# VectorE instead of negated copies and adding DMAs for one chunk's low parts, in a gated attention and GEGLU kernel

## The chip, the cores and the metric

The kernel runs on one core of a Trainium2 chip, as one program. The metric is the device time of one execution in microseconds; the median of three runs stands for a kernel. Names of engines: PE is TensorE, PEld its weight loads, DVE is VectorE, ACT is ScalarE, POOL is GpSimd, SP is SyncE.

## The reference

For 2048 tokens of width 512, two branches are computed from the same `x` and mixed by a sigmoid gate per token:

```python
x = A_x
g = _sigmoid((x * gate_w).sum(-1, keepdims=True))
a = _A_ref(x, A_wqkv, A_wo)        # 32 heads of 16; each token sees 8 keys, 2 apart
b = (_gelu(x @ w_gate) * (x @ w_up)) @ w_down     # F = 1792
return g * a + (1 - g) * b
```

All data is float32.

## The kernel before

**Numbers in two parts.** Each float32 operand of a matmul is held as a high part (a copy rounded to `F32R`) and a low part (the value less the high part). A product takes three matmuls: high by high, high by low, low by high.

**Two parities.** The tokens are split by parity into two halves of 1024. For each half the program makes queries and keys, then values, then runs the feed-forward branch over `FC` = 14 chunks of 128 hidden columns (`ffn(par)`, with `gate_up` per chunk). The products with `w_gate` and `w_up` use Strassen-Winograd sums over two token blocks, so a chunk has seven products (`product`, L781), and ends with two hidden tiles of 128 by 512, key `(f, 0)` and `(f, 1)`. `down` (L830) multiplies the hidden tiles of two chunks at a time by their rows of `w_down`; the last pair, chunks 12 and 13, is multiplied at the end of `ffn(1)`.

**Hidden tiles.** `hidden` (L797 to L807) multiplies GELU by up on VectorE (L797, tile `c`) and makes the two parts `hh` and `hl` in one of two ways. Where the chunk's number is not in `LOWS[par]`, ScalarE copies to `hh` (L800) and VectorE subtracts for `hl` (L801). Where it is, ScalarE writes the negated tile to `hl` (L805), a DMA that POOL issues adds the tile to it in memory (L806), and ScalarE copies to `hh` (L807).

**Attention beside it.** Attention runs on VectorE while TensorE does the feed-forward work. `pull` gives out its steps by a credit, behind the other work in priority. A unit is 128 channels of one parity. `mix` forms the value products (L585), folds them (L589, L591, L593), transposes half a unit (L598) and stores it by four DMAs on SP (L600). The second parity's last unit loads its values (`v`, L523 and L524) into the buffer of the unit before, so when that unit's last L585 is over.

**The end.** `out_first` multiplies the first parity's attention output by `wo` (L1062, tiles `A` and `S` as weights) while the second parity's units finish. `channels` loads half a unit back (L1040, `raw<-os`), splits it (ACT L90 for `hh`, DVE L91 for `hl`), and `finish` multiplies it into the accumulators. The program's last work is that chain for the last half unit, then four groups of three matmuls, a copy to `rt` or `s`, and the store of the output.

**Order.** A scheduler puts each engine's instructions in order from priorities and its own estimates of when operands are ready; at run time each engine takes them strictly in this order and waits on semaphores. A moved instruction can therefore move its neighbours.

Of the kernel before, what the change touches and what calls it, by code (L numbers as in the profile page):

```python
# [36 lines left out]
PIPE = 4  # L37
BT = 4
MASKED = -1e9 * DH ** 0.5
LOWS = (4, 8, 10), (4, 6, 8, 10, 12)  # L40


GROUPS = (("t1", "t2", "b11"), ("b21", "t3", "b22", "t4"))
# [5 lines left out]
def tile_gated_mix(ctx: ExitStack, tc: tile.TileContext, xt, wqkv, wff, wo, out):  # L49
# [11 lines left out]
    def tl(tag, dt=F32):  # L61
        return pool.tile([P, COLS.get(tag, 512)], dt, name=tag, bufs=BUFS[tag])
# [733 lines left out]
    def hidden(par, key, ge, up):  # L796
        nc.vector.tensor_tensor(ge, ge, up, op=OP.mult)  # L797
        hh_, hl_ = tl("hh", F32R)[:, :512], tl("hl", F32R)[:, :512]
        if key[0] not in LOWS[par]:
            END[:] = [nc.scalar.activation(hh_, ge, AF.Copy),  # L800
# [555 lines left out]
```

## Time and profile before

| quantity | value |
|---|---|
| median of three runs | 592.74 us (592.54 to 600.27) |
| profiled execution | 592.89 us, of which 591.1 us from the first to the last instruction |
| granted TensorE clock | 1.000 |
| busy: PE | 585.7 us (99%) |
| busy: DVE | 535.0 us (91%) |
| busy: ACT | 425.3 us (72%) |
| busy: POOL | 126.8 us (21%) |

The span is counted from the first instruction; 1.8 us of the profiled execution lie outside it. In the timeline, a row gives start, length, engine, line, operation, tiles and count, and in brackets the idle time of the engine ahead of the instruction and what ended it. An instruction's end can lie behind the next one's start, since an engine overlaps neighbours that don't wait for each other.

### The profile page before, as it was taken

Reading aid. Unit: us, or ns where it says so; the run is one execution under the profiler, and the core shown is the slowest. Engines: PE = TensorE matmul, PEld = TensorE weight load, DVE = VectorE, ACT = ScalarE, POOL = GpSimd, SP = SyncE. Lnnn points to the kernel's source line nnn. Section 1 sums busy time; section 2 is a strip of 40 time slices with the busy share of each in tenths; the row PEclk is TensorE's granted clock in tenths of the full one; section 3 lists DMA queues with packets and bytes.
Section 4 is the critical chain, followed back from the end, with each engine's and each line's share of the span. In section 5 each row is a group of like instructions: output and inputs, shape, how many; then the busy total and the mean of one; then the engine's idle time right before and its main releaser. Section 6 shows DMA issues by size and latency. Waiting matters only on the chain.

```text
span 591.1 us, 8266 instructions
## 1 busy us (share of the span) xinstructions
PE 585.7 (99%) x2743; PEld 489.1 (83%) x2743; DVE 535.0 (91%) x628; ACT 425.3 (72%) x752; POOL 126.8 (21%) x153
## 2 busy tenths in 40 slices
PE   9999999999999999999999999999999999999997
PEld 7889888888888888888889888888888888887885
DVE  6989998999899995998997999998999899989882
ACT  6778667778887779786687655768776967796522
POOL 0140751112111212113120761112121212112200
PEclk9999999999999999999999999999999999999999
DMA  8789999978987979899989999969798989548915
GB/s 305 228 247 281 301 310 231 296 197 238 289 222 218 273 205 273 224 264 347 284 231 380 222 272 269 277 162 257 178 263 224 254 213 247 144 111 227 202 44 178
DMA packets 87848, 141.71 MB, mean 240 GB/s; under 512 B 8575, under 2 KB 49919, under 8 KB 87806
## 3 DMA queue, kind: packets, MB, share of 16 engines
q1 hardware_dynamic: 65454, 103.21, 52.2%
q0 software_dynamic: 22064, 37.59, 34.6%
q8 instruction: 21, 0.34, 0.2%
q10 hardware_dynamic: 288, 0.39, 0.2%
q14 instruction: 21, 0.17, 0.1%
HBM read 69.83 MB, written 46.49 MB: 197 GB/s over the span
## 4 chain that ended last, share of the span: by engine, by line
PE 96%; ACT 2%; DMA 1%; issue 0%; SPq 0%; DVE 0%; ACTq 0%
PE p L781 44%; PE p L830 13%; PE acc L830 12%; PE acc L478 11%; PE p L1062 6%; PE p L364 4%; PE acc L364 3%; PE p L478 2%; PE acc L1062 2%; DMA raw<-xt 1%; ACT A L90 0%; ACT L898 0%; ACT g L135 0%; ACT hl L805 0%; ACT hh L807 0%
## 5 line engine op out<-in xcount | busy, mean ns | idle before, releaser
L781 PE MATMUL p<-S,g 128*128 128x512 f32 x672 | 167.0, 389 | 0.0
L781 PEld LDWEIGHTS p<-S,g 128*128 128x128 f32 x672 | 125.8, 188 | 25.8
L781 PE MATMUL p<-A,g 128*128 128x512 f32 x504 | 125.8, 389 | 0.0
L781 PEld LDWEIGHTS p<-A,g 128*128 128x128 f32 x504 | 94.4, 188 | 19.8 <-ACT rt L845 0.4
L585 DVE TENSOR_TENSOR prod<-v,lg 128x2048 f32<-128x2048 f32 x32 | 72.8, 2274 | 1.4 <-DMA v<-vs 1.2
L542 DVE TENSOR_REDUCE lg<-prod 128x128 f32<-128x2048 f32 x32 | 73.0, 2280 | 0.2
L539 DVE TENSOR_TENSOR prod<-kq 128x2048 f32<-128x2048 f32 x32 | 72.9, 2277 | 0.2
L830 PE MATMUL p<-d,hh 128*128 128x512 f32 x224 | 68.6, 390 | 0.3 <-ACT p L824 0.3
L830 PE MATMUL acc<-d,hh 128*128 128x512 f32 x224 | 59.7, 389 | 0.0
L740 POOL DMA_DIRECT2D g<-raw x26 | 23.6, 907 | 161.1 <-ACT g L737 103.6
L792 ACT ACTIVATE c<-p 128x512 f32<-128x512 f32 x56 | 33.4, 597 | 33.7 <-PE p L781 33.6
L830 PEld LDWEIGHTS p<-d,hh 128*128 128x128 f32 x224 | 41.9, 188 | 9.5 <-ACT p L824 0.8
L830 PEld LDWEIGHTS acc<-d,hh 128*128 128x128 f32 x224 | 42.0, 188 | 8.7
L793 DVE TENSOR_TENSOR c<-c,s 128x512 f32<-128x512 f32 x56 | 37.8, 681 | 5.5 <-ACT c L792 5.2
L830 PE MATMUL p<-d,hl 128*128 128x512 f32 x112 | 42.1, 389 | 0.0
L797 DVE TENSOR_TENSOR c<-c 128x512 f32<-128x512 f32 x56 | 38.1, 683 | 1.3 <-ACT c L898 1.2
L589 DVE TENSOR_TENSOR prod<-prod 128x1024 f32<-128x1024 f32 x32 | 39.0, 1217 | 0.1
L845 ACT ACTIVATE rt<-p 128x512 f32<-128x512 f32 x48 | 27.8, 596 | 15.0 <-PE p L830 14.8
L786 ACT ACTIVATE s<-p 128x512 f32<-128x512 f32 x56 | 33.2, 594 | 5.3 <-PE p L781 4.9
L478 PE MATMUL acc<-d,S 128*128 128x512 f32 x144 | 35.5, 390 | 0.1
L830 PE MATMUL acc<-d,hl 128*128 128x512 f32 x112 | 35.1, 389 | 0.0
L772 POOL DMA_DIRECT2D d<-r x23 | 19.8, 860 | 68.9 <-ACT d L771 41.6
(222 smaller groups left out, 1062.3 us busy)
## 6 DMA issues: line engine op xcount, KB each, us to landing
g<-raw POOLq DMA_DIRECT2D x26, 512.0 KB, 6.7
ws<-g SPq DMA_DIRECT2D x14, 768.0 KB, 5.9
g<-ws SPq DMA_DIRECT2D x14, 768.0 KB, 6.7
r<-wff SPq DMA_DIRECT2D x28, 256.0 KB, 4.4
raw<-wff SPq DMA_DIRECT2D x14, 512.0 KB, 4.6
d<-r POOLq DMA_DIRECT2D x23, 256.0 KB, 6.7
ws<-raw SPq DMA_DIRECT2D x14, 384.0 KB, 5.8
raw<-ws SPq DMA_DIRECT2D x14, 384.0 KB, 4.0
```

Source lines behind the costliest of these rows:

```text
L364: LAST[:] = [nc.tensor.matmul(ps[:, :n], x[:, ts], VO[b][w][:, kc * WQ:kc * WQ + n], start=first, stop=(kc == 1 and i == 2), skip_group_ch ...
L478: LAST[:] = [nc.tensor.matmul(ps, x[:, ts], w, start=(start and kc == i == 0), stop=(kc == 1 and i == 2), skip_group_check=True)]
L539: paced(nc.vector.tensor_tensor(prod, spans(k, jj), q[:, jj:jj + 2, None, :].to_broadcast([P, 2, W, UC]), op=OP.mult))
L542: nc.vector.tensor_reduce(two_of(lg, jj), prod.rearrange("p j w (h d) -> p (j w) h d", d=DH), axis=AX.X, op=OP.add)
L585: paced(nc.vector.tensor_tensor(prod.rearrange("p j w (h d) -> p (j w) h d", d=DH), spans(v, jj).rearrange("p j w (h d) -> p j w h d", d=D ...
L589: nc.vector.tensor_tensor(prod[:, :, :4], prod[:, :, :4], prod[:, :, 4:], op=OP.add)
L781: LAST[:] = [nc.tensor.matmul(ps, w_, a_, start=(start and kc == 0 and n == 0), stop=(kc == 1 and n == 2), skip_group_check=True)]
L792: nc.scalar.activation(c, ps, AF.Copy)
L793: nc.vector.tensor_tensor(c, c, s, op=OP.add)
L797: nc.vector.tensor_tensor(ge, ge, up, op=OP.mult)
L830: LAST[:] = [nc.tensor.matmul(pp, a[:, ts], w, start=(i == 0 and n == 0 and gr == 0), stop=(i == 1 and n == 2), skip_group_check=True)]
L1062: LAST[:] = [nc.tensor.matmul(pa, a, b, start=(first and n == 0), stop=(last and n == 2), skip_group_check=True)]
```

## The change

The number 12 is taken out of the second parity's list, so the two hidden tiles of its chunk 12 are split by VectorE as those of most chunks are.

```diff
-LOWS = (4, 8, 10), (4, 6, 8, 10, 12)
+LOWS = (4, 8, 10), (4, 6, 8, 10)
```

Two rows L805, two L806 and two L807 go; two rows L800 and two L801 come. On each engine the order is the same up to the end of chunk 12; from there the scheduler sets some rows otherwise. Three places matter.

First place: ScalarE, the second hidden tile of chunk 12, which is made while chunk 13 runs. `p<-rt` (L824) puts a partial sum back into a PSUM bank for `down`. Before:

```order
677 L90 ACTIVATE A<-raw 128x4x4x32
678 L882 ACTIVATE c<-p 128x512
679 L90 ACTIVATE A<-raw 128x4x4x32
680 L805 ACTIVATE hl<-c 128x512
681 L807 ACTIVATE hh<-c 128x512
682 L824 ACTIVATE p<-rt 128x512
683 L792 ACTIVATE c<-p 128x512
```

With the change:

```order
676 L90 ACTIVATE A<-raw 128x4x4x32
677 L800 ACTIVATE hh<-c 128x512
678 L882 ACTIVATE c<-p 128x512
679 L90 ACTIVATE A<-raw 128x4x4x32
680 L824 ACTIVATE p<-rt 128x512
681 L792 ACTIVATE c<-p 128x512
```

One copy instead of two stands ahead of L824 here, and one instead of two stood ahead of it for the first tile.

Second place: VectorE, the third value product (L585) of the last unit but one and the split of the first parity's output (L91, tile `S`) around it. Before:

```order
547 L593 TENSOR_TENSOR o<-prod 128x4x64
548 L91 TENSOR_TENSOR A<-raw,A 128x4x4x32
549 L793 TENSOR_TENSOR c<-c,s 128x512
550 L598 STREAM_TRANSPOSE tb<-o 128x512
551 L585 TENSOR_TENSOR prod<-v,lg 128x2048
552 L797 TENSOR_TENSOR c<-c 128x512
553 L793 TENSOR_TENSOR c<-c,s 128x512
554 L91 TENSOR_TENSOR S<-raw,S 128x4x4x32 x3
```

With the change:

```order
549 L801 TENSOR_TENSOR hl<-c,hh 128x512
550 L91 TENSOR_TENSOR A<-raw,A 128x4x4x32
551 L593 TENSOR_TENSOR o<-prod 128x4x64
552 L793 TENSOR_TENSOR c<-c,s 128x512
553 L91 TENSOR_TENSOR S<-raw,S 128x4x4x32
554 L793 TENSOR_TENSOR c<-c,s 128x512
555 L598 STREAM_TRANSPOSE tb<-o 128x512
556 L585 TENSOR_TENSOR prod<-v,lg 128x2048
```

The second new subtraction, one L91 and one L793 now stand ahead of this value product. Between it and the unit's fourth value product the same number of rows of this size stands as before: two L91 on `hl<-raw` have come ahead of the fourth, and these two have left.

Third place: VectorE, the last half unit. Before:

```order
581 L91 TENSOR_TENSOR hl<-raw,hh 128x4x4x32
582 L591 TENSOR_TENSOR prod<-prod 128x2x256
583 L593 TENSOR_TENSOR o<-prod 128x4x64
584 L91 TENSOR_TENSOR hl<-raw,hh 128x4x4x32
585 L585 TENSOR_TENSOR prod<-v,lg 128x2048
```

With the change:

```order
586 L591 TENSOR_TENSOR prod<-prod 128x2x256
587 L91 TENSOR_TENSOR hl<-raw,hh 128x4x4x32
588 L593 TENSOR_TENSOR o<-prod 128x4x64
589 L585 TENSOR_TENSOR prod<-v,lg 128x2048
```

The L91 that takes the unit's first half back stood behind L593 and stands ahead of it now.

## The prediction

> **What bounds the kernel now.** The page's busy times and its chain of work come first, then who TensorE waited for, then the timeline of the last 75 us.
>
> ```profile
> PE 585.7 (99%) x2743; PEld 489.1 (83%) x2743; DVE 535.0 (91%) x628; ACT 425.3 (72%) x752; POOL 126.8 (21%) x153
> ...
> PE 96%; ACT 2%; DMA 1%; issue 0%; SPq 0%; DVE 0%; ACTq 0%
> ```
>
> ```profile
> PE p L76 <- DVE warm L73: 1.0, 1, 1.0
> PE p L830 <- ACT p L824: 0.3, 1, 0.3
> ```
>
> TensorE is 99% busy and holds 96% of the chain. In 591.1 us it waited for other engines twice, 1.0 us at the very start and 0.3 us late. So work taken off ScalarE, POOL or the DMAs, or given to VectorE, counts only where it makes or removes a wait of TensorE. Nothing here can buy more than that 0.3 us and the last microseconds behind TensorE's last matmul.
>
> The one late wait lies behind ScalarE's queue, in the stretch of the change:
>
> ```profile
> 532.57 0.72 PE L830 MATMUL p<-d,hh 128*128 128x512 f32 x2 [0.33 <-ACT p L824]
> ```
>
> ```profile
> 520.77 0.62 ACT L805 ACTIVATE hl<-c 128x512 fp32r<-128x512 f32 x1
> 521.29 0.62 ACT L807 ACTIVATE hh<-c 128x512 fp32r<-128x512 f32 x1
> 521.81 0.62 ACT L90 ACTIVATE A<-raw 128x512 fp32r<-128x512 f32 x1
> ...
> 530.87 0.64 ACT L805 ACTIVATE hl<-c 128x512 fp32r<-128x512 f32 x1
> 531.39 0.64 ACT L807 ACTIVATE hh<-c 128x512 fp32r<-128x512 f32 x1
> 531.91 0.61 ACT L824 ACTIVATE p<-rt 128x512 f32<-128x512 f32 x1
> 532.43 0.60 ACT L792 ACTIVATE c<-p 128x512 f32<-128x512 f32 x1
> ```
>
> L824 ends at 532.52 and TensorE goes on at 532.57. No row here has a bracket: ScalarE came to L824 straight from the copies of the hidden tile, one each 0.52 us.
>
> **What leaves.** Two negated copies, 2 x 0.52 = 1.04 us of ScalarE's queue, one ahead of L824 by 11 us and one by 1 us. ScalarE may spend some of the first on waits between; the second is close. TensorE needs only 0.33. I take the whole stall as gone: **-0.33 us**; bounds: -0.33 and 0.
>
> The two adding DMAs leave too:
>
> ```profile
> 521.68 0.85 POOL L806 DMA_DIRECT2D hl<-c  x1 [11.00 <-ACT hl L805]
> 523.75 0.85 POOL L772 DMA_DIRECT2D d<-r  x1 [1.23 <-ACT d L771]
> 531.80 0.85 POOL L806 DMA_DIRECT2D hl<-c  x1 [7.20 <-ACT hl L805]
> ```
>
> ```profile
> hl<-c POOLq DMA_DIRECT2D x2, 256.0 KB, 4.5
> ```
>
> ```profile
> 557.65 0.39 PE L830 MATMUL acc<-d,hl 128*128 128x512 f32 x1
> ```
>
> POOL idles ahead of each and ahead of the next issue, L772, so that nothing in its queue moves up. The transfers land 4.5 us behind their issue, about 526 and 536; TensorE first needs these low parts at 557.65. That 21 us early becomes still earlier is worth 0. The cover would be gone only if the new subtractions came 26 us late.
>
> **What comes to VectorE.** Two subtractions. Their price is that of the 40 there are now:
>
> ```profile
> L801 DVE TENSOR_TENSOR hl<-c,hh x40: 673/683/693, 72.6 to 543.5; 128x512 fp32r<-128x512 f32 x40
> ```
>
> ```profile
> 520.41 0.69 DVE L562 TENSOR_REDUCE m<-lg 128x64 f32<-128x512 f32 x1 [1.44 <-ACT lg L557]
> 521.02 2.28 DVE L585 TENSOR_TENSOR prod<-v,lg 128x2048 f32<-128x2048 f32 x1
> ...
> 533.07 0.69 DVE L793 TENSOR_TENSOR c<-c,s 128x512 f32<-128x512 f32 x1 [0.97 <-ACT c L792]
> ...
> 534.30 2.25 DVE L585 TENSOR_TENSOR prod<-v,lg 128x2048 f32<-128x2048 f32 x1
> ...
> 541.22 0.68 DVE L801 TENSOR_TENSOR hl<-c,hh 128x512 fp32r<-128x512 f32 x1
> 541.82 0.68 DVE L797 TENSOR_TENSOR c<-c 128x512 f32<-128x512 f32 x1
> ...
> 544.08 2.28 DVE L585 TENSOR_TENSOR prod<-v,lg 128x2048 f32<-128x2048 f32 x1
> ...
> 552.49 2.29 DVE L585 TENSOR_TENSOR prod<-v,lg 128x2048 f32<-128x2048 f32 x1 [1.25 <-DMA v<-vs]
> ...
> 569.83 0.69 DVE L91 TENSOR_TENSOR hl<-raw,hh 128x512 fp32r<-128x512 f32 x1 [0.89 <-ACT hh L90]
> ...
> 575.20 0.71 DVE L598 STREAM_TRANSPOSE tb<-o 128x512 f32<-128x512 f32 x1
> 582.53 0.69 DVE L91 TENSOR_TENSOR hl<-raw,hh 128x512 fp32r<-128x512 f32 x1 [6.62 <-ACT hh L90]
> ```
>
> A subtraction lasts 0.68 us, but the next operation starts 0.60 behind its start (541.22 and 541.82); I charge 0.60. [...]
>
> How late is VectorE, place by place?
>
> First subtraction: it stands right behind L562, and waits for its high part, which takes L805's place and ends at 520.77 + 0.62 = 521.39. It starts near 521.45, the value product behind it at 522.05 instead of 521.02: +1.03.
>
> Second: +0.60. Then the 0.97 idle ahead of L793 goes, since L792 stands behind the same relieved ScalarE queue: -0.97. One L91 and one L793 now stand ahead of the third value product: 2 x 0.60 = +1.20. Together 1.03 + 0.60 - 0.97 + 1.20 = 1.86 us, less 0.2 or so if the pair of rows that waited before finds its operands ready. Up to the fourth value product the count of rows is the same, but three of them depended on ScalarE's copies; I take **+1.5** for that one, between 0.66 (had the extra pair stayed where it was) and 1.86.
>
> The last unit's values are loaded when it ends:
>
> ```profile
> 546.40 0.32 SPq L523 DMA_DIRECT2D v<-vs  x1
> ...
> 575.94 1.75 SPq L600 DMA_DIRECT2D os<-tb  x4
> ```
>
> It ends at 544.08 + 2.28 = 546.36, SP issues at 546.40, and VectorE idles 1.25 us for the landing. That wait doesn't absorb the delay, for it hangs on the same instruction: the load starts 1.5 later and lands 1.5 later. Behind the load on SP stand only the stores of this unit. From 552.49 to the transpose at 575.20 the one other wait is the 0.89 ahead of L91. L593 (0.42 us, and 0.04 to the next that waits for it) stood ahead of that wait and now stands behind it: +0.46. The last transpose is 1.5 + 0.46 = **1.96 us** later, at 577.16.
>
> **What is late next.** The last half unit is stored, loaded back, copied and subtracted; all of it follows the transpose.
>
> ```profile
> 581.87 0.63 ACT L90 ACTIVATE hh<-raw 128x512 fp32r<-128x512 f32 x1 [0.75 <-DMA raw<-os]
> ```
>
> ```profile
> 584.18 0.41 PEld L1062 LDWEIGHTS p<-S,hh 128*128 128x128 f32 x2
> 584.63 0.19 PEld L1062 LDWEIGHTS p<-S,hl 128*128 128x128 f32 x1
> ```
>
> ```profile
> 584.86 0.39 PE L1062 MATMUL p<-S,hl 128*128 128x512 f32 x1
> ...
> 586.89 0.39 PE L1062 MATMUL p<-S,hl 128*128 128x512 f32 x1
> ```
>
> Today the low part is ready at 582.53 + 0.69 = 583.22; its weights load at 584.63 and its matmul runs at 584.86: 1.41 to 1.64 us to spare. TensorE comes there 0.33 earlier with the old stall gone, so 1.08 to 1.31 remain. The chain comes 1.96 later: a new stall of 0.65 to 0.88. (The high part, ready at 582.50 for 584.18, is short too, inside that stall.) Behind it the tail is the same.
>
> **The sum:** -0.33 + 0.65 to 0.88 = +0.32 to +0.55; I take +0.45. Against the profiled execution that is a span of 591.1 + 0.45 = 591.55 and 593.3 us; that execution lies 0.15 above the median of 592.74, so **593.2 us** for the median.
>
> **Rivals.**
>
> *The cover holds.* If the fourth value product slips by 0.66 only, the transpose is 1.12 late, and the 1.08 to 1.31 cover it. Only the old stall goes: 592.74 - 0.33 = **592.4**. For it: the waits between may swallow more than I granted. Against: the two rows that now stand ahead.
>
> *Slower, VectorE bounds the end.* If ScalarE's relief doesn't reach L792 (its operand comes from TensorE), the 0.97 stays, and the delay reaches the transpose in full: 1.96 + 0.97 = 2.93, a stall of 2.93 - 1.31 = 1.62 at the least and 1.85 at the most, less the 0.33: +1.29 to +1.52, **594.1**. It decides as soon as the last low part is later than 584.3. For it: VectorE is nearly unbroken from 552 to 576. Against: L792 starts 0.52 behind L824 with no bracket, so it was the queue. [...]
>
> *The new order hurts elsewhere.* The list only moves priorities; a matmul group of TensorE could meet an operand that isn't there, say the `S` parts, which VectorE splits among the rows that moved.
>
> ```profile
> 540.62 0.68 DVE L91 TENSOR_TENSOR S<-raw,S 128x512 fp32r<-128x512 f32 x1
> ```
>
> ```profile
> 546.32 1.52 PE L1062 MATMUL p<-g,S 128*128 128x512 f32 x6
> ```
>
> These have 5 us to spare, so 1.9 of delay doesn't reach them; some other operand, late by one or two VectorE rows more than it has, would cost 0.6 to 1.2 us: about 594.
>
> **How the numbers follow.** Forecast 0.58, cover holds 0.22, VectorE bounds the end 0.14, elsewhere 0.06. The range takes in the first three, and the 0.2 that the two undisturbed runs lie apart: 592.4 - 0.2 = 592.2 up to 594.1 + 0.3 = 594.4. 2% is 11.9 us, about what a measurement of this kernel can tell from no change. Faster by that is excluded but for surprise, since TensorE alone is busy 585.7 us: 0.01. Slower would take a chain 13 us late; the largest delay here is 3: 0.03. Within: 0.96.
>
> **What would show it.** TensorE's 0.33 wait for L824 is gone; a new wait on `hh` or `hl`, from L90 or L91, of 0.6 to 0.9 us in the last 8 us; the last transpose near 577 (less 0.3 if the whole end comes earlier); POOL has no L806 behind chunk 10; VectorE busy about 1.4 us more. A last transpose below 576.5, or a TensorE without waits at the end, makes the forecast wrong towards 592.4; a stall over 1.5 us, or one in another stage, makes it wrong upwards.

## The result, and the profile after

The changed kernel takes 597.02 us in the median of 22 runs (595.12 to 606.1), the kernel before 593.4 us beside it (22 runs, 592.37 to 600.27). The ratio is 1.005, with a 95% interval of 1.0027 to 1.0073; ratios leave out the executions of a slower state (here 605.3 and 606.1 us), so they need not be the quotient of the two medians. The change makes the kernel slower by less than 2%; its time is above the forecast of 593.2 and above the range's end at 594.4. The interval tells 0.5% from no change, finer than the 2% that the prediction supposed. In a second set of runs (e1_again below) it was 599.07 against 592.89, a ratio of 1.011, interval 1.0077 to 1.0144.

Who TensorE waited for, first profile of the changed kernel (total us, times, longest):

```profile
PE acc L830 <- DMA hl<-c: 3.3, 1, 3.3
PE p L1062 <- ACT hh L90: 3.2, 1, 3.2
PE acc L830 <- ACT hh L800: 1.8, 1, 1.8
PE p L76 <- DVE warm L73: 1.0, 1, 1.0
```

The two waits of L830 stand at 391 and 412 us, more than 100 us ahead of the first changed instruction. The profile of e8 below, an edit of the kernel before, has such a wait of 3.1 us at 410 us too. The second profile of the changed kernel lacks them (span 596.6 us, 598.4 us in all), so it is the one read from here on (the "second profile"). Its waits, and its chain of work by engine:

```profile
PE p L1062 <- ACT hh L90: 4.2, 1, 4.2
PE p L76 <- DVE warm L73: 1.0, 1, 1.0
```

```profile
PE 87%; DVE 5%; DMA 3%; ACT 2%; issue 1%; SPq 0%; ACTq 0%; DVEq 0%
```

The wait for L824 is gone, and one wait in the last 8 us has come, on the high part (`hh`, L90) of the last half unit. These are the two places that were named. VectorE, at 0% of the chain before, has 5% now, and the DMAs have gone from 1% to 3%. The size is what is off: 4.2 us, not 0.65 to 0.88.

VectorE in the second profile, at the places of the sum:

```profile
517.48 0.69 DVE L793 TENSOR_TENSOR c<-c,s 128x512 f32<-128x512 f32 x1
...
520.95 0.69 DVE L801 TENSOR_TENSOR hl<-c,hh 128x512 fp32r<-128x512 f32 x1 [0.32 <-ACT hh L800]
521.56 2.29 DVE L585 TENSOR_TENSOR prod<-v,lg 128x2048 f32<-128x2048 f32 x1
...
532.99 0.69 DVE L793 TENSOR_TENSOR c<-c,s 128x512 f32<-128x512 f32 x1
...
535.42 2.25 DVE L585 TENSOR_TENSOR prod<-v,lg 128x2048 f32<-128x2048 f32 x1
...
545.08 2.29 DVE L585 TENSOR_TENSOR prod<-v,lg 128x2048 f32<-128x2048 f32 x1
...
556.54 2.29 DVE L585 TENSOR_TENSOR prod<-v,lg 128x2048 f32<-128x2048 f32 x1 [5.50 <-DMA v<-vs]
...
579.62 0.71 DVE L598 STREAM_TRANSPOSE tb<-o 128x512 f32<-128x512 f32 x1
```

The row to look at is the one at 556.54: before, the same product waited 1.25 us for the last unit's values, now 5.50. From the fourth value product (545.08, before 544.08) VectorE is 1.00 late, from that wait on 4.05 (556.54 against 552.49), and at the last transpose 4.42 (579.62 against 575.20).

The wait is the load itself. Its two parts by size with the time from issue to landing, before and then after:

```profile
v<-vs SPq DMA_DIRECT2D x1, 512.0 KB, 5.6
v<-vs SPq DMA_DIRECT2D x1, 448.0 KB, 4.5
```

```profile
v<-vs SPq DMA_DIRECT2D x1, 512.0 KB, 8.7
v<-vs SPq DMA_DIRECT2D x1, 448.0 KB, 7.1
```

In the first profile it is 8.0 and 6.4. What else moves at that time: POOL's adding writes of the output (L1080), before:

```profile
545.60 0.86 POOL L1080 DMA_DIRECT2D out<-s  x1 [2.68 <-ACT s L1079]
547.50 0.86 POOL L1080 DMA_DIRECT2D out<-r  x1 [1.04 <-ACT r L1079]
```

and after, with the load's issue on SP behind them:

```profile
544.92 0.85 POOL L1080 DMA_DIRECT2D out<-s  x1 [3.11 <-ACT s L1079]
546.39 0.85 POOL L1080 DMA_DIRECT2D out<-r  x1 [0.62 <-ACT r L1079]
549.11 0.86 POOL L1080 DMA_DIRECT2D out<-s  x1 [1.86 <-ACT s L1079]
```

```profile
547.40 0.34 SPq L523 DMA_DIRECT2D v<-vs  x1
```

The load is issued 1.00 later (before 546.40), and the write `out<-r` 1.11 earlier. So a write that stood 1.10 behind the load stands 1.01 ahead of it. The DMA queues in the fourth and fifth microsecond behind the load's issue (q1 is the loads' queue, q0 POOL's; packets, MB, share of 16 engines), before and after:

```profile
q1 hardware_dynamic: 212, 0.76, 104.9%
q0 software_dynamic: 5, 0.00, 0.1%
```

```profile
q1 hardware_dynamic: 121, 0.42, 65.7%
q0 software_dynamic: 69, 0.12, 38.4%
```

Before, the load has the engines to itself in these 2 us and moves 0.76 MB of its 0.98. After, POOL's packets run among its own, and it moves 0.42.

The copy of the last half unit's high part on ScalarE, and the end of TensorE's work, after:

```profile
586.93 0.63 ACT L90 ACTIVATE hh<-raw 128x512 fp32r<-128x512 f32 x1 [6.92 <-DMA raw<-os]
```

```profile
583.06 0.39 PE L1062 MATMUL acc<-S,hl 128*128 128x512 f32 x1
587.61 1.22 PE L1062 MATMUL p<-S,hh 128*128 128x512 f32 x2 [4.16 <-ACT hh L90]
588.63 0.63 PE L1062 MATMUL p<-S,hl 128*128 128x512 f32 x1
...
592.47 0.43 PE L1062 MATMUL p<-S,hl 128*128 128x512 f32 x1
```

The last four groups take 592.47 - 587.61 = 4.86 us from their first start to their last, before 586.89 - 584.40 = 2.49 (the pair `hh` of the first group started at 584.40). The windows of the second profile say why; the last columns are the granted clock, the DMA share and GB/s:

```profile
584.00:587.60 3.60, 0.00 (x0) 0.00 (x0) 0.01 (x1) 0.67 (x2) 0.00 (x0) 0.74 0.68 219
587.60:590.00 2.40, 2.39 (x6) 1.86 (x7) 1.28 (x2) 1.04 (x2) 0.00 (x0) 0.50 0.40 154
```

While TensorE waits, its granted clock falls to 0.50, and the last groups, behind it, take about twice their time. Together: the last groups start 587.61 - 584.40 = 3.21 late, and take 2.37 longer, 5.58 for the last matmul. The span grew by 5.5. The second part differs between executions: of the 22 timed runs, the five with a mean clock of 0.999 took 595.12 to 596.47 us, the three with 0.994 took 597.70 to 599.24.

### The profile page after: what moved, and what is told of

Read it like the earlier page. It is cut to its first block, busy times and chain, and to the rows that moved or that the text cites. A ratio compares the mean times of both kernels' runs of the same rounds, so it can differ in the third digit from the quotient of the medians.

```text
span 603.5 us, 8260 instructions
## 1 busy us (share of the span) xinstructions
PE 590.4 (98%) x2743; PEld 492.4 (82%) x2743; DVE 536.5 (89%) x630; ACT 424.5 (70%) x750; POOL 125.1 (21%) x151
## 4 chain that ended last, share of the span: by engine, by line
PE 82%; DVE 5%; DMA 5%; issue 4%; ACT 2%; SPq 0%; POOL 0%; ACTq 0%; DVEq 0%; POOLq 0%
PE p L781 40%; PE acc L830 11%; PE acc L478 11%; PE p L830 10%; PE p L364 3%; PE acc L364 3%; DVE prod L585 2%; PE p L478 2%; DMA hl<-c 2%; DMA v<-vs 1%; DMA raw<-os 1%; PE p L1062 1%; DVE prod L589 1%; DMA os<-tb 1%; PE p L76 1%
## 5 line engine op out<-in xcount | busy, mean ns | idle before, releaser
L585 DVE TENSOR_TENSOR prod<-v,lg 128x2048 f32<-128x2048 f32 x32 | 72.8, 2274 | 5.1 <-DMA v<-vs 4.9
L830 PE MATMUL p<-d,hh 128*128 128x512 f32 x224 | 68.5, 389 | 0.0
L830 PE MATMUL acc<-d,hh 128*128 128x512 f32 x224 | 59.9, 390 | 1.8 <-ACT hh L800 1.8
L830 PEld LDWEIGHTS acc<-d,hh 128*128 128x128 f32 x224 | 42.0, 188 | 10.9 <-ACT hh L800 2.2
L830 PEld LDWEIGHTS p<-d,hh 128*128 128x128 f32 x224 | 42.2, 188 | 8.8
L793 DVE TENSOR_TENSOR c<-c,s 128x512 f32<-128x512 f32 x56 | 37.9, 682 | 5.9 <-ACT c L792 5.5
L830 PE MATMUL p<-d,hl 128*128 128x512 f32 x112 | 42.1, 389 | 0.0
L830 PE MATMUL acc<-d,hl 128*128 128x512 f32 x112 | 35.7, 395 | 3.3 <-DMA hl<-c 3.3
```

The costliest lines, as they stand in the source:

```text
L585: paced(nc.vector.tensor_tensor(prod.rearrange("p j w (h d) -> p (j w) h d", d=DH), spans(v, jj).rearrange("p j w (h d) -> p j w h d", d=D ...
L793: nc.vector.tensor_tensor(c, c, s, op=OP.add)
L830: LAST[:] = [nc.tensor.matmul(pp, a[:, ts], w, start=(i == 0 and n == 0 and gr == 0), stop=(i == 1 and n == 2), skip_group_check=True)]
```

## The experiments

Three theories were to be told apart. **The load**: it goes out beside POOL's writes, takes longer, and VectorE's lateness reaches TensorE's end. **The order alone**: the two subtractions and the moved rows make VectorE late by themselves. **The clock**: the wait is small, and the half clock behind it is most of the loss. Ratios are against the kernel before in the same set of runs, with 95% intervals. Some diffs are shortened, or spread over more lines for reading.

**The changed kernel again** (e1_again), with no edit.

> The changed kernel once more, for a profile of an execution without the stalls near 391 and 412 us that its first profile has. Theory of the late chain: TensorE still waits for the last high part at the end, by 1 us or more, and the granted clock is 0.5 over its last twelve matmuls (12 x 0.2 = 2.4 us more); ratio 1.004 to 1.007. Rival of the stalls in the middle: without them the end shows the 0.6 to 0.9 us of wait that the prediction had and no half clock, 593 to 594 us, and only the executions with a stall in the middle are slower.

599.07 us (6 runs), ratio 1.011 (1.0077 to 1.0144). It is the profile read above. The loss is real, and both of its parts show. The median is 2.05 us above that of the first set, and why the two sets differ stays open; three of these six runs have a mean clock of 0.993 or 0.994.

**Last unit's values in another buffer** (e2_kq_after on the changed kernel, e3_kq_before on the kernel before). Queries and keys are done by then, so their buffer is free, and the load needn't wait for the fourth value product.

```diff
-        VT[par, u] = v = pool.tile([P, 2 * NP - 1, UC], F32, name="v")
+        VT[par, u] = v = (pool.tile([P, 3 * NP - 1, UC], F32, name="kq")[:, :2 * NP - 1]
+                          if (par, u) == (1, NU - 1) else pool.tile([P, 2 * NP - 1, UC], F32, name="v"))
```

> The changed kernel with the last unit's values in the key and query buffer, which is free by then, so that their load needn't wait for the unit before. Late chain: VectorE's wait for the values (4.87 us in the first profile) is gone, the last transpose is 3 to 5 us earlier, TensorE doesn't wait at the end, the clock stays at 1.0, and the time is that of the kernel before or 0.3 us less, ratio 0.998 to 1.001. Rival of the stalls in the middle: the end doesn't matter, ratio stays 1.004 to 1.006.

> The kernel before with the same buffer for the last unit's values, for the gain that this edit has by itself. Late chain: TensorE didn't wait at the end of the kernel before, so VectorE comes 1.2 us earlier and TensorE no earlier, ratio 0.999 to 1.001. Rival, that the kernel before also loses time at its end in its ordinary runs: ratio under 0.998.

e2: 592.21 us (12 runs), ratio 0.9998 (0.9978 to 1.0018). e3: 592.88, ratio 0.9996 (0.9973 to 1.002). The load of e2 on SP, then VectorE and TensorE:

```profile
506.88 0.32 SPq L523 DMA_DIRECT2D kq<-vs  x1
```

```profile
545.37 2.30 DVE L585 TENSOR_TENSOR prod<-v,lg 128x2048 f32<-128x2048 f32 x1
...
551.26 2.25 DVE L585 TENSOR_TENSOR prod<-kq,lg 128x2048 f32<-128x2048 f32 x1
...
575.03 0.71 DVE L598 STREAM_TRANSPOSE tb<-o 128x512 f32<-128x512 f32 x1
```

```profile
583.60 0.62 PE L1062 MATMUL p<-S,hh 128*128 128x512 f32 x2
```

The fourth product is as late as in the changed kernel (545.37), both subtractions are there, and yet the last transpose is where it was in the kernel before (575.03 against 575.20) and the end has no wait: neither the product at 551.26 nor the first of the last four groups (583.60, before 584.40) has a bracket. So the order alone shows no cost once the load is out of it. This is the lowest median of all, but its interval holds 1, as does that of the same edit on the kernel before; a gain over the kernel before isn't shown.

**Idle matmuls in TensorE's wait** (e4_warm_after 24 of them, e5_warm72 72), into a bank that is free, ahead of the last four groups:

```diff
+            if jj == BT:
+                idle = bank("acc0")
+                for i in range(72): # 24 in the first
+                    nc.tensor.matmul(idle[:, i % 4 * P:(i % 4 + 1) * P], warm, warm, start=True, stop=True)
             add(NU - 1, jj)
```

> The changed kernel with 24 matmuls of zeros, 128 columns each (about 2.6 us at full clock), on TensorE ahead of the last four groups, into a bank that is done with; they change no result. Late chain with a slow clock: they stand where TensorE waited, so they cost nothing, the clock stays at 1.0 to the end, and 1.5 to 2.4 us are won, ratio 1.000 to 1.003. Rival, that the wait alone makes the loss: nothing won, ratio 1.004 to 1.006. Rival of the stalls in the middle: these 2.6 us are added to a short wait, ratio 1.007 or more.

> The changed kernel with 72 of the idle matmuls instead of 24 (0.056 us each as the last run showed, so 4.0 us) ahead of the last four groups; they change no result. With 24 TensorE still idled 2.6 us and the clock was 0.5 for 3.4 us behind it. If the half clock comes from TensorE's idling, it now stays at 1.0 to the end and the twelve last matmuls take 2.7 us instead of 5.1: 1.5 to 2.5 us under the changed kernel of the same day, 595 to 596.5. If the half clock has another source, nothing is won: 597 to 599.

e4: 597.79 us, ratio 1.0095 (1.0064 to 1.0125). The 24 filled 1.5 us, less than the 2.6 meant (at the program's start, L76, 31 of this shape start from 1.0 to 4.2, 0.107 us apart, and 24 x 0.107 = 2.6). A wait of 2.6 stayed, and the half clock with it (0.50 from 588 to 590): this one decided nothing. e5: 596.45, ratio 1.0065 (1.0043 to 1.0088), with this end on TensorE and this copy of the high part on ScalarE:

```profile
584.23 4.19 PE L1102 MATMUL acc<-warm 128*128 128x128 bf16 x72
588.24 0.70 PE L1062 MATMUL p<-S,hh 128*128 128x512 f32 x2
...
590.86 0.39 PE L1062 MATMUL p<-S,hl 128*128 128x512 f32 x1
```

```profile
586.71 0.63 ACT L90 ACTIVATE hh<-raw 128x512 fp32r<-128x512 f32 x1 [5.77 <-DMA raw<-os]
```

```profile
588.00:590.00 2.00, 2.00 (x16) 1.70 (x14) 0.77 (x3) 0.60 (x1) 0.00 (x0) 1.00 0.59 229
```

The groups run at a granted clock of 1.00 again, 590.86 - 588.24 = 2.62 us instead of 4.86. With TensorE kept at work the clock stayed at 1.00, and behind the idle 4.16 us of the second profile it was 0.50: in these two profiles the half clock goes with TensorE's idling. The groups still start 588.24 - 584.40 = 3.84 late, and not all of that is the wait: the high part is there at 586.71 + 0.63 = 587.34, and the idle matmuls keep TensorE 0.9 us past it. What the half clock costs in the medians isn't settled by this run, since the changed kernel's own median was 599.07 in one set and 597.02 in another, 0.6 above e5. The runs of the first set by their clock say more: with a mean clock of 0.999 the changed kernel still takes 1.7 to 3.1 us more than the 593.4 of the kernel before. The clock alone doesn't explain the loss.

**The moved splits put back** (e6_order_back): the two subtractions stay, and the `L91` rows that came ahead of the third and fourth value products go behind them again. `behind` is a dependency of order only.

```diff
-        split(nc.vector, *by_t, o.rearrange("p (a t j) -> p a t j", a=4, t=BT))
+        ins = split(nc.vector, *by_t, o.rearrange("p (a t j) -> p a t j", a=4, t=BT))
+        behind(ins.ins, M[1, NU - 2, 4]) # first parity's second half; M[...6] for the second parity's units 0 and 1
```

> The changed kernel with the splits of loaded channels put back behind the third and the fourth value product of the last unit but one, as in the kernel before; both new subtractions stay. The value load then starts 1.2 us earlier than in the changed kernel. Theory that the moved rows make the loss: the load goes out ahead of the second output write again, lands in 6 us instead of 8.7, and TensorE waits 0 to 1 us at the end, 592.3 to 594. Rival, that the subtractions' own time makes it: the wait stays at 2 us or more, 595 to 598.

596.42 us, ratio 1.0057 (1.0035 to 1.0079). The time was expected to recover and didn't. The rows say why (SP, POOL, VectorE):

```profile
546.77 0.34 SPq L523 DMA_DIRECT2D v<-vs  x1
```

```profile
546.85 0.85 POOL L1080 DMA_DIRECT2D out<-r  x1 [0.63 <-ACT r L1079]
```

```profile
556.23 2.29 DVE L585 TENSOR_TENSOR prod<-v,lg 128x2048 f32<-128x2048 f32 x1 [4.61 <-DMA v<-vs]
```

The load is 0.63 earlier than in the changed kernel, but the write is issued 0.08 behind it, not 1.1. The load's parts took 7.1 and 9.0, and the wait stayed. TensorE waited 3.33 us for the last high part.

**The writes left out** (e9_no_write), and **one write held back** (e7_hold_out) until VectorE's transpose behind the load:

```diff
-                nc.gpsimd.dma_start(out_v[2 * jj], r, accum_op=OP.add)
+                jj in (2, 3, 4) or nc.gpsimd.dma_start(out_v[2 * jj], r, accum_op=OP.add) # e9
+                put = nc.gpsimd.dma_start(out_v[2 * jj], r, accum_op=OP.add) # e7
+                # in words: for jj == 3, put waits for the L598 of the last unit but one, second half
```

> The changed kernel without the adding writes of output tiles 2, 3 and 4 (left out: those rows of the output keep their first part only); the order on every other engine is the same. These are the writes beside the value load. If they slow the load: it lands in 5 to 6 us instead of 7.7 to 9.0, VectorE's wait for it is 1 to 2.5 us instead of 4.6 to 5.5, TensorE's wait at the end 0.5 to 1.5 us, no half clock ahead of its last matmul, 592.9 to 594, which is what the prediction's sum had. If the load is slow for another reason: 7.5 us or more, 596 to 599.

> The changed kernel with the fourth adding write of the output, which POOL issues 1 us ahead of the value load, held until VectorE's transpose behind that load; nothing else moves. Theory that the two transfers share the DMA engines and the write in front delays the load: the load lands in 5 to 6.5 us instead of 8.7, VectorE's wait for it falls from 5.5 to 2.5 us or so, TensorE's wait at the end from 4.2 to 1.5 or less; 592.5 to 595. Rival, that the load is slow for another reason: its time stays at 8 us or more, 597 to 599.

e9: 592.7 us, ratio 1.0003 (0.9978 to 1.0028). The load's landing, and VectorE:

```profile
v<-vs SPq DMA_DIRECT2D x1, 512.0 KB, 4.3
v<-vs SPq DMA_DIRECT2D x1, 448.0 KB, 3.5
```

```profile
545.89 2.28 DVE L585 TENSOR_TENSOR prod<-v,lg 128x2048 f32<-128x2048 f32 x1
...
552.96 2.29 DVE L585 TENSOR_TENSOR prod<-v,lg 128x2048 f32<-128x2048 f32 x1 [1.12 <-DMA v<-vs]
...
576.11 0.71 DVE L598 STREAM_TRANSPOSE tb<-o 128x512 f32<-128x512 f32 x1
```

This is the sharpest of the runs. The load goes out at 548.19, as late as in the changed kernel (the whole execution runs 0.8 later, from ahead of the change on), VectorE's order is the changed one, and without the writes the load takes 4.3 instead of 8.7 and the time is that of the kernel before. (The kernel leaves part of the output out, so it serves for the time only.) e7: 595.12, ratio 1.003 (1.0 to 1.006); its load took 6.0 and 6.8, and VectorE waited 3.64. In the rows, one write less gives back part; in the ratios that is clear only against the second set of the changed kernel.

**One tile at a time** (e8_first_only, tile `(12, 0)`; e10_second_only, tile `(12, 1)`), on the kernel before:

```diff
-        if key[0] not in LOWS[par]:
+        if key[0] not in LOWS[par] or (par, key) == (1, (12, 0)): # (12, 1) in the other
```

> The kernel before with the change for the first hidden tile of chunk 12 alone. One subtraction instead of two, no L91 row ahead of the fourth value product, but one L91 ahead of the third, and the later order of the end. If each subtraction costs its 0.6 to 1 us: the value load 0.5 to 1.2 us later than before, still ahead of or beside the output write, the end's wait 0 to 1.5 us, 592.5 to 595. If the collision of the load with the write decides: as in the changed kernel, a load of 8 us or more and a wait over 3 us, 596 to 598.

> The kernel before with the change for the second hidden tile of chunk 12 alone, the counterpart of the run with the first tile alone (593.54). One subtraction more; no row of L91 has come ahead of the fourth value product. Theory that the loss starts where the load comes beside the write: the load is 0.3 to 0.9 us later, still ahead of the write by 0.4 us or more, lands in 6.5 us or less, the end's wait is 0 to 1 us, 592.5 to 594; the two halves of the change cost under 1.5 us together where the whole costs 3 or more. Rival, that each subtraction has a fixed price: 594.5 or more.

e8: 593.54, ratio 1.0004 (0.9978 to 1.0031). e10: 592.84, ratio 1.0005 (0.998 to 1.0031). Neither half has a price clear of noise (the intervals allow 1.8 us for either), and in neither profile does TensorE wait 1 us or more at the end; both together cost 3.6 to 6.2 us in the medians. That, and the rows below, read as a threshold and not as a sum of two prices: the load's longer part took 5.6 us before, 6.4 and 5.5 with one tile and 8.7 with both. The load in the profiles in which it goes out behind the fourth value product, with the nearest writes of POOL counted from its issue (those of e7, e8 and the changed kernel's first profile are of executions with waits near 400 us, ahead of these rows):

| kernel | writes issued | parts took, us | VectorE waited |
|---|---|---|---|
| before | -0.80, +1.10 | 4.5, 5.6 | 1.25 |
| second tile alone | -0.79, +1.03 | 4.6, 5.5 | 1.13 |
| first tile alone | -0.79, +0.61 | 4.6, 6.4 | 2.00 |
| splits put back | -1.40, +0.08 | 7.1, 9.0 | 4.61 |
| changed | -2.48, -1.01, +1.71 | 7.1, 8.7 | 5.50 |
| changed, first profile | -2.48, -1.00, +1.72 | 6.4, 8.0 | 4.87 |
| changed, 24 idle matmuls | -2.48, -1.00, +1.72 | 6.4, 8.6 | 5.44 |
| changed, 72 idle matmuls | -2.48, -1.00, +1.72 | 6.1, 7.7 | 4.57 |
| changed, one write held | -2.47, +1.73 | 6.0, 6.8 | 3.64 |
| changed, writes left out | none | 3.5, 4.3 | 1.12 |

With the second write 1.0 to 1.1 behind the load, the load's longer part takes 5.5 to 5.6; with it 0.6 behind 6.4, 0.08 behind 9.0, and 1.0 ahead 7.7 to 8.7. Why a write 0.8 ahead does little in the first rows, and a pair 2.5 and 1.0 ahead does much, the packets show only in part. In the kernel before, POOL sends 65 packets in the third microsecond behind the load's issue, in which the load's first 37 come; then 5 in the two microseconds in which the load sends 212; then 75 in the sixth, beside 39 of the load's last. So the early write is nearly through when the load starts, and the later one starts when the load is nearly over. What orders them in the DMA engines wasn't tried.

## Why the prediction was wrong

Point by point, against the second profile:

| step | as predicted | measured |
|---|---|---|
| TensorE's wait for L824 | gone | gone |
| idle ahead of L793 | 0.97, gone | gone (532.99) |
| first value product behind the subtraction | +1.03 | +0.54; +1.01 counted from L793, which starts 0.47 earlier in this execution (517.48, before 517.95), ahead of the change |
| third value product | +1.86, or 0.2 less | +1.12; +1.59 so counted |
| fourth value product | +1.5 | +1.00; +1.47 so counted |
| load of `v` | "starts 1.5 later and lands 1.5 later" | issued 1.00 later, takes 3.1 longer |
| rows behind L593 | +0.46 | 4.42 - 4.05 = +0.37 |
| last transpose | 577.16 | 579.62 |
| new wait in the last 8 us | 0.65 to 0.88, on `hh` or `hl` | 4.16, on `hh` |
| the last four groups | "the tail is the same" | +2.37 |

The working on VectorE held: counted from L793 at 517.48, every shift up to the fourth value product, and the one behind L593, is within 0.3 us of what was predicted. The old wait, the chain from VectorE to the last half unit and the place of the new wait were right too.

The step that failed first is the sentence that the load "starts 1.5 later and lands 1.5 later". It took a transfer's duration as fixed while its start moved against POOL's writes. Counted from the row at 517.48, the load came 1.47 later and the write 1.11 - 0.47 = 0.64 earlier, of which TensorE's old wait for L824 is 0.33; between the two that is 2.11 us. Leaving the writes out (a load of 4.3 us, 592.7) shows that this is the cause, and with the load out of VectorE's way (592.21) the later rows alone show no cost. The traces show the load and the writes sharing the 16 DMA engines: in the two microseconds above, 69 of POOL's packets and 121 of the load's took 38.4% and 65.7% of the engines' time, 104.1% together, where 5 and 212 had taken 0.1% and 104.9%. The prediction counted the queues of SP that the load passes, but not the DMA engines that it shares.

The second failure follows from the first: "the tail is the same" was said for a wait of 0.65 to 0.88 us, and the tail stood behind one of 4.16, at a granted clock of 0.50. Its measured price is 2.37 us in the second profile, and 4.86 - 2.62 = 2.24 against the run with 72 idle matmuls; the executions with a mean clock of 0.999 hardly paid it. None of the rivals had either. "VectorE bounds the end" came nearest, with the right direction and the right chain, but its condition didn't hold (the 0.97 ahead of L793 did go), and at 594.1 it had no more than VectorE's own rows to add. What the forecast had summed shows in e9, without the writes: there the last four groups take 586.98 - 584.09 = 2.89 us, 0.40 more than before, for a short wait on the last low part, where 0.65 to 0.88 was forecast.

The sum as it should have been, on the second profile: the high part is 586.93 - 581.87 = 5.06 later than before. Of this, 4.42 is the last transpose (1.00 the product, 3.05 the longer load, 0.37 the order behind it) and 0.64 the way through memory. The spare time was 584.40 - 582.50 less the 0.05 between L90 and its matmul, 1.85; 5.06 - 1.85 = 3.21 late, and 2.37 of half clock.

## What to carry to other kernels

When a change shifts an instruction that a buffer's load hangs on, look at what other queues send in the microseconds around the new issue: here the same 512 KB took 4.3 us with no write beside them and 5.5 to 9.0 with writes. Then ask how long the bounding engine would idle at worst, for here more than the wait was lost: with waits of 4.16, 2.62 and 2.10 us (second profile, e4 and e7) the granted clock fell to 0.50, and the last four groups took 2.37, 1.64 and 1.98 us longer than in the kernel before; with one of 3.33 (e6) it was 1.00 over these groups, and they took 0.40 longer. Where a load is tied to the last read of a buffer just ahead of a critical chain, another free buffer takes the whole question away (592.21 us in e2).

## What the runs showed of the hardware

The half clock lasted 6.8 us in the second profile of the changed kernel, and 3.4 us in e7 and e4. The granted clock by fifths of a microsecond, at the fall and at the return, in the second profile and in e7:

```profile
585.60:585.80 0.20, 0.00 (x0) 0.00 (x0) 0.00 (x0) 0.00 (x0) 0.00 (x0) 0.79 0.52 195
...
592.40:592.60 0.20, 0.20 (x2) 0.00 (x0) 0.00 (x0) 0.10 (x1) 0.00 (x0) 0.65 0.97 379
```

```profile
591.80:592.00 0.20, 0.20 (x2) 0.16 (x2) 0.20 (x1) 0.00 (x0) 0.00 (x0) 0.89 0.00 0
...
595.20:595.40 0.20, 0.20 (x2) 0.11 (x2) 0.00 (x0) 0.19 (x1) 0.00 (x0) 0.58 0.00 0
```

From the shares, the clock of 0.50 lasted from 585.72 to 592.54, 6.8 us, and from 591.96 to 595.37, 3.4 us. In e4 it was 3.4 us again, from 587.75 to 591.16. In e7 TensorE had waited only 2.10 us and was at work for 0.84 us when the clock fell. In e6, behind a wait of 3.33 us, the clock was 1.00 until 592.40, and TensorE's last matmul ended at 590.14 + 0.39 = 590.53. So a wait's length alone didn't decide, and what else did isn't shown.
